# Two-operand sums made by accumulating DMA transfers from GpSimd instead of a tensor-tensor add

## The chip, the cores and the metric

The kernel runs on one core of a Trainium2 chip. Times are device microseconds (us) of that core, from the first to the last thing that the program does there. The engines are TensorE (PE in the profile; its weight loads are PEld), VectorE (DVE), ScalarE (ACT), GpSimd (POOL) and SyncE (SP), which issues the DMA transfers. Each engine works through its own list of instructions in order, and waits on semaphores that the others, or a landed transfer, raise.

## What is computed

Two independent layers of 2048 rows and width 1024, put side by side in the output. A is attention with 32 heads of 32 columns and a projection; B is a Fourier mixing by dense matrices, with the real part kept. All data is float32.

```python
def _A_ref(x, wqkv, wo):
    qkv = ((x @ wqkv).reshape(B, S, 3, H, Dh)).transpose(2, 0, 3, 1, 4)
    q, k, v = qkv[0], qkv[1], qkv[2]
    p = softmax(einsum("bhqd,bhkd->bhqk", q, k) * Dh ** -0.5)
    o = einsum("bhqk,bhkd->bhqd", p, v)
    return o.transpose(0, 2, 1, 3).reshape(B, S, D) @ wo

def _B_ref(x, dft_seq_re, dft_seq_im, dft_hid_re, dft_hid_im):
    a = einsum("bsd,ed->bse", x, dft_hid_re)
    b = einsum("bsd,ed->bse", x, dft_hid_im)
    return einsum("ts,bse->bte", dft_seq_re, a) - einsum("ts,bse->bte", dft_seq_im, b)

out = concatenate([_A_ref(...), _B_ref(...)], axis=-1)
```

## The kernel before

**The dense products.** Every dense product (QKV, the two Fourier products `dense1` and `dense2`, the projection) is done by a seven-product scheme on quarters of its operands, in the manner of Strassen and Winograd. The products are numbered 1 to 7, and each takes as operands a quarter or a signed sum of quarters. In QKV they run as products 1, 2, 5, 6, 3, then 7 and 4; in the others as `ORDER`, 1, 2, 6, 7, 5, 3, 4. Lists such as `w_terms`, `x_terms`, `a_terms` and `b_terms` give for each product the terms of an operand: a sign, a source in DRAM, and what has to have been written before. Product 5's stationary operand is `(+q10, +q11)`, product 6's is `(+q10, +q11, -q00)`. Of the moving operands, product 6's in `dense1` and `dense2` has a third term with a plus sign.

An operand is split into two float32r parts, high and low (`halves`: a cast at L527 on ACT or L528 on DVE, and a subtraction at L531 on POOL or DVE), and a product is three matmuls for each pair of tiles (L421, or L443 where three groups are interleaved).

**How an operand is fetched.** `fetch` (L465 and after) loads the first term into a tile `raw` (in the first stage `er`) of 128 x 512 float32, 256 KB, by a DMA on SP (L491). For every further term that lies in DRAM it loads a second tile `g` (in the first stage `raw`) by another DMA on SP (L500), and combines the two by one elementwise instruction, L507, which may go to POOL or to DVE. Then come the cast and the subtraction. Rings of buffers limit how far ahead the loads run: six `raw`, four `g`, four pairs of high and low for stationary operands.

**Attention.** For each head, scores are made twice: with queries on the partitions (`psS`, L1322) for the row maxima (DVE, L1328) and row sums (ACT, L1331), and transposed (`psT`, L1447), with an exponential on ACT (L1456), as the operand of the product with V (L1479). This goes on from about 240 us to about 2750 us, and the matmuls of the dense products are set between.

**The order.** The order of all engines is written out when the program is built, by a list scheduler, `Plan`. It plays the kernel through with assumed durations: it starts an operation when its operands are ready, charges a transfer 256 KB at 360 KB per us (`KB_US`) and 1.6 us more until it lands (`LANDING`), and lets POOL and DVE read a landed tile no sooner than 2 us after that (`MARGIN`). It also keeps POOL's elementwise instructions and those of DVE marked `two` from overlapping (`port`, `choose`), and where they come near each other adds a dependency (`behind`). PE takes dense matmuls where the attention has nothing ready, and in proportion to what is done of it. The plan fixes only the order; on the chip every instruction waits for what it needs.

Of the kernel before, what the change touches and what calls it, by code (L numbers as in the profile page):

```python
# [11 lines left out]
ALU = mybir.AluOpType  # L12
# [11 lines left out]
NB = 512  # L24
NPT, NPT2 = 23, 8
H2 = 8
NRAW, NHL, NG = 6, 4, 4
WARM = 10
NE, NCR = 4, 4
PEND = 1  # L30
# [36 lines left out]
class Plan:  # L67
# [26 lines left out]
    def op(self, engine, cost, emit, after=(), uses=(), rank=0.0, kb=0, order=None, other=None, lanes=1, two=False):  # L94

        o = Op(engine, cost, emit, rank, kb, other, two)
        o.lanes = lanes
        seen = set()  # L100
        for d in after:
            if d is not None and id(d) not in seen:
                seen.add(id(d))
                self._wait(o, d)
        for u in uses:
            u.append(o)
        if order is not None:
            p, order.first = order.first, o
            if p is not None and not p.begun:
                p.soon.append(o)  # L110
                o.left += 1
        if o.left == 0:
            self._release(o)
        return o

    def _wait(self, o, d):
        if d.end is None:
            d.then.append(o)
            o.left += 1
        else:  # L120
            o.ready = max(o.ready, self.after(d, d.engine, o))
            if d.engine == "SP":
                o.landed = max(o.landed, d.end)

    def after(self, d, e, o):
# [8 lines left out]
    def start(self, o, e=None):  # L134
        e = e or o.engine
        made = o.emit(e) if o.other else o.emit()
        o.begun = True
        self.free[e] = self.now + (o.cost if e == o.engine else o.other[1])
        if e == "POOL" or e == "DVE" and o.two:
            self.port = self.free[e]  # L140
        if e == "DVE" and o.two:
            self.held = made, self.free[e]
        elif e == "POOL" and self.held is not None and self.held[1] > self.now - self.NEAR:
            self.behind(made, self.held[0])
        if o.kb:
            for _ in range(o.lanes):
                t = max(self.free[e], self.lane[0])
                self.dma = max(self.dma, t) + o.kb / o.lanes / self.KB_US
                o.end = self.dma + self.LANDING
                self.lane = self.lane[1:] + [o.end]  # L150
                if o.lanes > 1:
                    self.free[e] = t + o.cost
        else:
            o.end = self.free[e]
            self.free[e] -= self.OVERLAP.get(e, 0.0)
        for t in o.then:
            t.ready = max(t.ready, self.after(o, e, t))
            if e == "SP":
                t.landed = max(t.landed, o.end)
            t.left -= 1  # L160
            if t.left == 0:
                self._release(t)
        for t in o.soon:
            t.ready = max(t.ready, self.now)
            t.left -= 1
            if t.left == 0:
                self._release(t)
        o.then = o.soon = ()
        o.emit = None
# [56 lines left out]
def kernel(  # L226
# [11 lines left out]
    nc = tc.nc  # L238
# [143 lines left out]
    NEAR = 0.2  # L382
    SFIRST = 0.3
    ADD = 0.68
    FILL = 3 * (7 * 24 * 4 + 7 * 16 * 4 + 7 * 8 * 16 + 2 * 8 * 4)
    ATT = H * (128 * MM + 16 * PV) + (3 * H2 + 2 * (H - H2)) * SWITCH

# [2 lines left out]
    op = pl.op  # L390
# [66 lines left out]
    def seq():  # L457
        return float(len(frees))
# [10 lines left out]
    def fetch(shape, terms, store=None, keep=None):  # L469

        box = {}
        raws, seconds, tile_of, gate = where[0]
        rank = seq()
        sign, *first = terms[0]
        loaded = len(first) == 2
        if len(terms) == 1 and not loaded:
            return first[0].get, first[0].made, first[0].users
        if keep is None:
            old, users = raws.take()
        else:  # L480

            old, users = gate + keep.users, keep.users

        def dest():
            if "r" not in box:
                box["r"] = tile_of(shape, "raw", len(raws.users)) if keep is None else keep.get()
            return box["r"]

        last = None
        if loaded:  # L490
            last = op("SP", ISSUE, lambda: nc.sync.dma_start(dest(), first[0]), old + first[1] + gate, [users], rank, 256, raws if keep is None else None)  # L491
            old = []
        for sign, *term in terms[1:]:
            other = {}
            if len(term) == 2:
                gold, gusers = seconds.take()

                def load(src=term[0], other=other):
                    other["q"] = tile_of(shape, "g", len(seconds.users))
                    nc.sync.dma_start(other["q"], src)  # L500

                q = op("SP", ISSUE, load, gold + term[1] + gate, [gusers], rank, 256, seconds)
            else:
                other["k"], q, gusers = term[0], term[0].made, term[0].users

            def add(e, sign=sign, other=other, a=None if last is not None else first[0]):
                return (nc.gpsimd if e == "POOL" else nc.vector).tensor_tensor(  # L507
                    out=dest(), in0=dest() if a is None else a.get(), in1=other["q"] if "q" in other else other["k"].get(), op=ALU.add if sign > 0 else ALU.subtract)

            last = op("POOL", SUB, add, old + [first[0].made if last is None else last, q], [users, gusers] + ([first[0].users] if last is None else []),  # L510
                      rank, 0, raws if keep is None and last is None else None, other=("DVE", ADD, 20 + rank), two=True)
            old = []
        if keep is not None:
            keep.made = last
        if store is not None:
            store[1].append(op("SP", ISSUE, lambda: nc.sync.dma_start(store[0], dest()), [last], [users], rank, 256))
        return dest, last, users
# [3 lines left out]
    def halves(raw, made, users, hi, lo, old, mine, order=(None, None)):  # L521
# [11 lines left out]
        a = op("DVE", CAST, high, [made] + old[0], [users, mine[0]], 10 + rank, 0, order[0], ("ACT", ACAST, 25 + rank) if spare[0] else None, two=True)  # L533
        b = op("POOL", SUB, low, [a] + old[1], [users, mine[0], mine[1]], rank, 0, order[1], other=("DVE", ADD, 25 + rank), two=True)
        return a, b

    def piece(terms, store=None):

        box = {}
        raw, made, users = fetch([P, 4, P], terms, store)  # L540
        (o0, u0), (o1, u1) = HR.take(), LR.take()

        def tile_of(key):
            def get():
                if key not in box:
                    box[key] = parts.tile([P, 4, P], F32R, name=key, tag=key, bufs=NHL)
                return box[key]
            return get

        h, l = tile_of("h"), tile_of("l")  # L550
        made = halves(raw, made, users, h, l, (o0, o1), (u0, u1), (HR, LR))
        both = Both(u0, u1)
        return Piece(h, l, made, both)
# [67 lines left out]
    def qkv():  # L621
# [128 lines left out]
        def gather(p, g, result, early, scale=None):  # L750
# [21 lines left out]
            def finish(ps, last):  # L772
# [43 lines left out]
                def put_u3(o):  # L816
                    if whole_u3:
                        u3[g] = (U2[0], U2[1], o)
                    else:
                        u_st[g][1].append(op("SP", ISSUE, lambda: nc.sync.dma_start(u_d[g][1], U2[0]()), [o], U2[1], rank, 256))  # L820

                if g < 2 * PAIRS or g >= 16:
                    def third(r, made, users):

                        o = op("POOL", SUB, lambda e: (nc.gpsimd if e == "POOL" else nc.vector).tensor_tensor(out=U2[0](), in0=r(), in1=U2[0](), op=ALU.subtract),
                               [made, U2[2]], [users, *U2[1]], rank, other=("DVE", ADD, 20 + rank), two=True)
                        put_u3(o)
# [130 lines left out]
    def add_op(emit, after, users, rank):  # L958
        return op("POOL", SUB, emit, after, users, rank, other=("DVE", ADD, 20 + rank), two=True)

# [595 lines left out]
    while nf < len(fills) or any(place[n] < len(s) for n, s in streams.items()):  # L1556
# [4 lines left out]
        if visit:  # L1561
            o = visit[0]
# [25 lines left out]
        for n, (o, h, k, *_) in heads.items():  # L1588
# [14 lines left out]
            rank = {"V": 0, "T": 1, "S": 0.5 if stock > SFIRST else 1.5}[n]  # L1603
            if n == "S" and "T" in heads and heads["T"][0].left == 0:
# [4 lines left out]
                if lead > 0:  # L1609
                    rank = 2  # L1610
            ok.append((rank, n))
        fill = None
        if nf < len(fills):
            o, first, left = fills[nf]
# [5 lines left out]
            elif ready < 1e17:  # L1620
                times.append(ready + LATE)
        if fill is not None and (not ok or (not first and left <= HB) or nf / (FILL - RES) <= done / ATT):
            pl.start(fill)
# [5 lines left out]
        if ok:  # L1629
            n = min(ok)[1]  # L1630
            o = heads[n][0]
# [48 lines left out]
```

## Time and profile before

| | us |
|---|---|
| three runs, median | 2942.45 |
| three runs, lowest to highest | 2941.8 to 2943.91 |
| profiled execution, span from first to last instruction | 2940.6 |
| PE busy in it | 2931.5 |
| DVE, ACT, POOL busy | 2275.1, 2271.7, 956.6 |

The page of the profile gives the profiled execution by its span alone; the runs' median lies 1.85 us above that span and the fastest run 1.2 us. The granted clock of TensorE is 1.000 throughout. The page's parts are read in this order: busy time by engine, the span in 40 slices, the DMA queues, the chain of work that ended last, then the groups of instructions by line.

### The profile page before, as it was taken

How to read it: one execution, taken by the hardware profiler on the slowest of the kernel's cores; microseconds unless marked ns; L12 is line 12 of the kernel's file. 1: busy time of each engine (PE TensorE's matmuls, PEld its weight loads, DVE VectorE, ACT ScalarE, POOL GpSimd, SP SyncE). 2: the span in 40 equal slices, each digit the busy share in tenths (PEclk: the TensorE clock that was granted, in tenths of full speed). 3: DMA queues.
4: the chain of work that ended last, by engine and by line, in shares of the span. 5: the costliest groups of instructions: out<-in, count | busy, mean ns of one | idle time of the engine just before them, and what ended most of it. 6: DMA issues, size and time to landing. Idle time of an engine off the chain costs nothing.

```text
span 2940.6 us, 45778 instructions
## 1 busy us (share of the span) xinstructions
PE 2931.5 (100%) x14922; PEld 2151.9 (73%) x14922; DVE 2275.1 (77%) x3103; ACT 2271.7 (77%) x4322; POOL 956.6 (33%) x746
## 2 busy tenths in 40 slices
PE   9999999999999999999999999999999999999999
PEld 7887777677777777777777777777777777677787
DVE  6778888788877877877677888787787788886685
ACT  5348888888888888888888888888888888886331
POOL 2323435222204432231112454433112454454142
PEclk9999999999999999999999999999999999999999
DMA  9975658666637655675434776655434786665753
GB/s 348 356 249 183 200 183 276 227 213 225 218 103 229 217 176 164 212 226 166 158 101 147 239 231 205 189 180 169 129 113 132 216 270 200 194 182 191 264 194 126
DMA packets 393880, 587.96 MB, mean 200 GB/s; under 512 B 112782, under 2 KB 114574, under 8 KB 393518
## 3 DMA queue, kind: packets, MB, share of 16 engines
q1 hardware_dynamic: 393644, 585.05, 61.8%
q8 instruction: 120, 1.97, 0.3%
q14 instruction: 116, 0.95, 0.1%
HBM read 421.30 MB, written 163.59 MB: 199 GB/s over the span
## 4 chain that ended last, share of the span: by engine, by line
PE 98%; DVE 1%; DMA 1%; ACT 0%; SPq 0%; issue 0%; DVEq 0%; ACTq 0%
PE pd L421 44%; PE psT L1447 16%; PE psS L1322 16%; PE pd L1479 15%; PE psT L421 6%; DVE negm L1328 0%; DMA er<-in_xa 0%; DVE l L531 0%; DMA qs<-qk_d 0%; PE psT L443 0%; ACT psS L1331 0%; DVE h L528 0%; PE pd L443 0%; ACT slot L527 0%; DVE slot L531 0%
## 5 line engine op out<-in xcount | busy, mean ns | idle before, releaser
L1328 DVE TENSOR_REDUCE negm<-psS 128x1 f32<-128x1024 f32 x1024 | 1242.8, 1221 | 226.4 <-PE psS L1322 215.2
L1331 ACT ACTIVATE psS<-psS,negm 128x1024 f32<-128x1024 f32 x1024 | 1223.9, 1195 | 71.8 <-DVE negm L1328 70.0
L421 PE MATMUL pd<-slot,h 128*128 128x512 f32 x3360 | 1144.0, 390 | 0.0
L1456 ACT ACTIVATE pt<-psT 128x512 f32<-128x512 f32 x1296 | 782.6, 697 | 260.1 <-PE psT L1447 237.2
L1447 PE MATMUL psT<-qs,ks 128*128 128x512 f32 x2048 | 794.3, 394 | 1.3 <-DMA qs<-qk_d 1.3
L421 PEld LDWEIGHTS pd<-slot,h 128*128 128x128 f32 x3360 | 630.7, 188 | 132.0
L421 PE MATMUL pd<-slot,l 128*128 128x512 f32 x1680 | 654.6, 390 | 0.0
L507 POOL TENSOR_TENSOR raw<-raw,g 128x512 f32<-128x512 f32 x295 | 382.6, 1304 | 483.8 <-DVE l L531 63.8
L1447 PEld LDWEIGHTS psT<-qs,ks 128*128 128x128 f32 x2048 | 381.8, 188 | 137.3 <-issue 45.3
L1322 PE MATMUL psS<-ks,qs 128*128 128x512 f32 x1552 | 473.4, 390 | 1.2 <-ACT psS L1331 1.2
L531 POOL TENSOR_TENSOR l<-raw,h 128x512 fp32r<-128x512 f32 x157 | 202.5, 1290 | 554.6 <-PE psT L1447 236.6
L531 POOL TENSOR_TENSOR slot<-raw,slot 128x512 fp32r<-128x512 f32 x156 | 201.0, 1293 | 518.0 <-DVE slot L528 146.3
L421 PEld LDWEIGHTS pd<-slot,l 128*128 128x128 f32 x1680 | 315.3, 188 | 67.0 <-issue 0.8
L1479 PE MATMUL pd<-pt,vt 128*32 128x512 f32 x2592 | 345.8, 594 | 0.0
L1322 PEld LDWEIGHTS psS<-ks,qs 128*128 128x128 f32 x1552 | 290.8, 188 | 64.0 <-ACT psS L1331 3.8
L1331 ACT ACTIVATION_READ_ACCUMULATOR psS<-psS,negm 128x1 f32 x1024 | 321.6, 314 | 0.0
L1456 ACT ACTIVATE ptm<-psT 128x512 f32<-128x512 f32 x392 | 242.6, 715 | 49.7 <-PE psT L1447 46.7
L1456 ACT ACTIVATE ptl<-psT 128x512 f32<-128x512 f32 x360 | 223.5, 708 | 31.0 <-PE psT L1447 30.2
L1479 PEld LDWEIGHTS pd<-pt,vt 128*32 128x32 f32 x2592 | 89.4, 110 | 180.3 <-issue 168.2
L421 PE MATMUL pd<-slot,slot 128*128 128x512 f32 x768 | 193.0, 391 | 0.0
L421 PEld LDWEIGHTS pd<-slot,slot 128*128 128x128 f32 x768 | 144.1, 188 | 31.2
L528 DVE CAST h<-raw 128x512 fp32r<-128x512 f32 x321 | 149.1, 467 | 14.5 <-PE pd L421 12.3
(139 smaller groups left out, 2323.8 us busy)
## 6 DMA issues: line engine op xcount, KB each, us to landing
raw<-in_ct SPq DMA_DIRECT2D x224, 256.0 KB
g<-in_ct SPq DMA_DIRECT2D x128, 256.0 KB
c<-u_d SPq DMA_DIRECT2D x120, 256.0 KB
qk_d<-e SPq DMA_DIRECT2D x52, 512.0 KB
qs<-qk_d SPq DMA_DIRECT2D x128, 192.0 KB
ks<-qk_d SPq DMA_DIRECT2D x128, 192.0 KB
raw<-ab_d SPq DMA_DIRECT2D x96, 256.0 KB
g<-ab_d SPq DMA_DIRECT2D x80, 256.0 KB
```

What stands on the lines that cost most here:

```text
L421: nc.tensor.matmul(box["ps"], a[1]((a[0].hi, a[0].lo)[u]()), b[1]((b[0].hi, b[0].lo)[v]()), start=k == 0, stop=k == n - 1)
L507: return (nc.gpsimd if e == "POOL" else nc.vector).tensor_tensor(out=dest(), in0=dest() if a is None else a.get(), in1=other["q"] if "q" i ...
L528: return nc.vector.tensor_copy(hi(), raw())
L531: return (nc.gpsimd if e == "POOL" else nc.vector).tensor_tensor(out=lo(), in0=raw(), in1=f(hi()), op=ALU.subtract)
L1322: nc.tensor.matmul(p[:, i * NB : i * NB + NB], (QX[0] if own else QS[h % 2])[:, qt * P : qt * P + P], KS[h % 2][:, c * 1024 + i * NB : c * ...
L1328: nc.vector.tensor_reduce(out=ST["negm"][:, c, qt : qt + 1], in_=box["p"], axis=AX.X, op=ALU.max, negate=True)
L1331: nc.scalar.activation(box["p"], box["p"], AF.Exp, bias=ST["negm"][:, c, qt : qt + 1], accum_out=ST["sums"][:, c, qt : qt + 1])
L1447: nc.tensor.matmul(box["p"], KS[h % 2][:, t * P : t * P + P], QS[h % 2][:, j * NB : j * NB + NB], start=True, stop=True)
L1456: nc.scalar.activation(box["t"], box["p"], AF.Exp)
L1479: nc.tensor.matmul(po["p"][j * DH : j * DH + DH, :], VT[h][:, k, :], box["t"], start=(k == t0), stop=(k == t), tile_position=(0, j * DH),)
```

## The change

In `fetch`, a further term that has a plus sign, lies in DRAM, and is added to a first term that was loaded too, no longer takes a tile of its own and an elementwise addition. GpSimd issues a DMA with `accum_op=add` from DRAM onto the first tile. The operation waits for the first tile's load (and for what wrote the term), and the later steps wait for its landing. Terms with a minus sign, and sums with a tile that is kept on the chip, stay as they were.

The scheduler learns the new kind of operation: it costs POOL 1.0 us (`DGE`), then counts as a transfer of 256 KB on the same DMA budget as SP's, without one of SP's eight lanes; it doesn't hold the port that POOL and DVE share, and no dependency of the `behind` kind is added for it. What follows it is treated as following a landed transfer.

Room: the ring of `g` tiles goes from four to three, and the space for descriptors of GpSimd's transfers from 256 to 1024 bytes of each partition.

```diff
-NRAW, NHL, NG = 6, 4, 4
+NRAW, NHL, NG = 6, 4, 3
@@ Plan._wait
-            if d.engine == "SP":
+            if d.kb:
                 o.landed = max(o.landed, d.end)
@@ Plan.start
-        if e == "POOL" or e == "DVE" and o.two:
+        if e == "POOL" and not o.kb or e == "DVE" and o.two:
             self.port = self.free[e]
...
-        elif e == "POOL" and self.held is not None and self.held[1] > self.now - self.NEAR:
+        elif e == "POOL" and not o.kb and self.held is not None and self.held[1] > self.now - self.NEAR:
             self.behind(made, self.held[0])
-        if o.kb:
+        if o.kb and e == "POOL":
+            self.dma = max(self.dma, self.free[e]) + o.kb / self.KB_US
+            o.end = self.dma + self.LANDING
+        elif o.kb:
...
-            if e == "SP":
+            if o.kb:
                 t.landed = max(t.landed, o.end)
@@ constants
+    DGE = 1.0
+    ACC = [True]
@@ fetch
             other = {}
+            if len(term) == 2 and sign > 0 and loaded and ACC[0]:
+                last = op("POOL", DGE, lambda src=term[0]: nc.gpsimd.dma_start(dest(), src, accum_op=ALU.add), [last] + term[1], [users], rank, 256)
+                continue
             if len(term) == 2:
                 gold, gusers = seconds.take()
@@ kernel
-    nc = bacc.Bacc("TRN2", target_bir_lowering=False, num_devices=1, dynamic_dma_scratch_size=256)
+    nc = bacc.Bacc("TRN2", target_bir_lowering=False, num_devices=1, dynamic_dma_scratch_size=1024)
```

## The prediction

> **What bounds the kernel now.** I read the page first (busy time, chain, DMA), then PE's own waits, then the table of stretches of 100 us and of 10 us, then the chain in order of time.
>
> ```profile
> span 2940.6 us, 45778 instructions
> PE 2931.5 (100%) x14922; PEld 2151.9 (73%) x14922; DVE 2275.1 (77%) x3103; ACT 2271.7 (77%) x4322; POOL 956.6 (33%) x746
> PE 98%; DVE 1%; DMA 1%; ACT 0%; SPq 0%; issue 0%; DVEq 0%; ACTq 0%
> ```
>
> PE is busy for 2931.5 of 2940.6 us and makes 98% of the chain. A busy PE need not be a PE at its pace, so I check that busy time hides no waiting:
>
> ```profile
> 2852.52 5.44 PE pd L421 x24
> 1970.98 7.00 PE pd L1479 x64
> L1479 PE MATMUL pd<-pt,vt 128*32 128x512 f32 x2592 | 345.8, 594 | 0.0
> L1479 PE MATMUL pd<-ptl,vt 128*32 128x512 f32 x720 | 136.8, 593 | 0.0
> L1479 PE MATMUL pd<-ptm,vt 128*32 128x512 f32 x784 | 125.5, 593 | 0.0
> L1555 PE MATMUL pd<-qs 96*128 96x512 f32 x10 | 4.6, 644 | 1.5 <-DVE qs L303 1.5
> ```
>
> In the last stage, where nothing but dense products is left, a matmul starts every 5.44 / 24 = 0.2267 us; a matmul with V starts every 7.00 / 64 = 0.1094 us. Of the 14922 matmuls, 2592 + 720 + 784 = 4096 are with V, 10 are a warm-up, and 10816 are of the first kind: 10816 x 0.2267 + 4096 x 0.1094 = 2452.0 + 448.1 = 2900.1 us. The warm-up is 4.6 us, and the plan's own price of changing to the products with V, 0.363 us for each of 8 x 3 + 24 x 2 = 72 visits, makes 26.1 us. Together 2930.8 of the 2931.5 us busy. PE runs at its pace, and the change takes no matmul away.
>
> So only PE's idle time, 2940.6 - 2931.5 = 9.1 us, can be won. Where does it lie?
>
> ```profile
> 0.00:10.00 10.00, 8.54 (x27) 6.61 (x28) 4.02 (x7) 5.27 (x8) 5.68 (x8) 1.00 0.75 241
> 10.00:20.00 10.00, 8.67 (x37) 6.58 (x37) 9.10 (x16) 8.94 (x15) 1.28 (x1) 1.00 0.96 341
> 2900.00:2940.00 40.00, 36.84 (x163) 30.18 (x161) 13.47 (x20) 2.51 (x4) 2.62 (x3) 1.00 0.26 99
> PE psT L443 <- DVE acc L799: 1.3, 1, 1.3
> PE psT L1447 <- DMA qs<-qk_d: 1.3, 1, 1.3
> PE psS L1322 <- ACT psS L1331: 1.2, 3, 0.5
> ```
>
> The columns of a stretch are its length, then busy us (and count) of PE, PEld, DVE, ACT, POOL, then granted clock, DMA share and GB/s. The first 20 us lose 1.46 + 1.33 = 2.8 us, before any sum that the change touches is wanted (they belong to products 5 and 6; the first products are 1 and 2). The end loses 3.2 us, the last result's way out, and 0.6 us past 2940. That leaves 9.1 - 2.8 - 3.2 - 0.6 = 2.5 us in between: the second and third of these waits, 1.3 + 1.2. The change can gain at most these 2.5 us, less than a tenth of a per cent. What it can lose isn't bounded so.
>
> **The change, part by part.** A difference of 0.2%, 5.9 us, is about what a measurement of this kernel can tell from none.
>
> How many sums: the rule takes terms with a plus sign behind a loaded first term. Products 5 and 6 have one each in a stationary operand: QKV 8 weight blocks x 2 and 4 value blocks x 2 = 24; `dense1` 8 x 2 = 16; `dense2` 2 halves x 16 tiles x 2 = 64. The moving operand of product 6 has one: 8 in `dense1`, 16 in `dense2`. The projection has none (its plus terms go with tiles kept on chip). Sum 24 + 16 + 64 + 24 = 128. Of them 7 + 7 = 14 fall in QKV's first stage (3 weight blocks and 4 value blocks for each product), 114 beside the attention.
>
> *Removed: 128 additions at L507.*
>
> ```profile
> 0.00:2940.00 2940.00, 110.01 (x146) 407.35 (x314) 1.00 0.62 200
> L507 POOL TENSOR_TENSOR raw<-raw,g 128x512 f32<-128x512 f32 x295 | 382.6, 1304 | 483.8 <-DVE l L531 63.8 <-issue 48.2 <-DMA raw<-in_xb 44.9
> L500 SPq DMA_DIRECT2D g<-in_ct x128: 327/376/1986, 1600.7 to 2580.3; - x128
> ```
>
> In the first row stand busy us (and count) of DVE and of POOL at L507. There are 146 + 314 = 460; at the same shares, 128 are about 87 on POOL (87 x 1.297 = 113 us) and 41 on DVE (41 x 0.753 = 31 us). On engines busy 33% and 77% of the span, beside a PE that doesn't wait for them, that is worth nothing. SP issues 128 loads fewer, at 0.376 us median 48 us of its time; also off the path.
>
> *Added: 128 issues on POOL.* GpSimd issues no transfer in this trace, so the price is bounded: from below by an issue on SP, 0.33 us, from above by POOL's own pass over such a tile, 1.30 us. I take 1.0, the plan's price, which lies by the upper row. That is 128 us, against 113 removed; nothing on the path.
>
> *Added: one more read on the DMA engines.* A sum reads the tile it writes: 128 x 256 KB = 33.6 MB.
>
> ```profile
> q1 hardware_dynamic: 393644, 585.05, 61.8%
> 1700.00:1800.00 100.00, 100.00 (x521) 72.96 (x513) 81.46 (x108) 85.04 (x165) 50.68 (x39) 1.00 0.70 219
> 2300.00:2400.00 100.00, 100.00 (x505) 73.86 (x504) 84.46 (x111) 89.05 (x171) 55.74 (x44) 1.00 0.78 246
> 110.00:120.00 10.00, 10.00 (x46) 8.29 (x45) 5.31 (x10) 4.11 (x7) 2.05 (x2) 1.00 0.99 337
> 150.00:160.00 10.00, 10.00 (x45) 8.26 (x45) 5.99 (x9) 2.72 (x5) 3.81 (x3) 1.00 0.74 246
> ```
>
> Beside 585 MB it is 6% (nothing, if the read costs no time of its own; 61.8% to 65.4%, if it costs as a write does). In the attention's heaviest stretches, products 5 and 6 of `dense2`, the engines stand at 0.70 and 0.78, and it is hidden. In the first 150 us they stand at about 1.0: a rival, below.
>
> *Moved: the sum from "two loads side by side, then an add" to "a load, then a transfer".* In the plan the cast may start, after the first load has landed and 2 us passed, 1.0 + 256/360 + 1.6 + 2.0 = 5.3 us later, against 1.3 us or 0.7 us for an addition. POOL waits for the first load at the head of its queue, and behind it stand the low halves (L531) and the subtractions; it waits so now as well (44.9 us before L507 for `in_xb` alone). The tile is held about 4 us longer in a ring of six; at 24 operands in about 100 us of a product each of the six may be held 25 us. `g` going from four to three costs nothing where half of the stationary operand's seconds no longer use it.
>
> *The wait that counts* is that of the cast on DVE, because behind it stand the row maxima, for which ACT waits, which frees `psS`, for which PE waits. Now:
>
> ```profile
> L528 DVE CAST slot<-raw 128x512 fp32r<-128x512 f32 x228 | 103.1, 466 | 8.7 <-DMA raw<-ab_d 4.4 <-POOL raw L507 3.8
> L507 DVE TENSOR_TENSOR raw<-raw,g 128x512 f32<-128x512 f32 x77 | 55.5, 728 | 3.3 <-POOL raw L507 1.8 <-DMA g<-in_ct 1.3 <-issue 0.2
> ```
>
> DVE waits 4.4 + 3.8 + 1.8 + 1.3 = 11.3 us for loads and sums, and PE waits 1.2 us on ACT's `psS`: about 0.11 us of PE for each us of DVE. That is an estimate from few cases, but the only one here. I take it that one in eight of the 114 transfers comes 1 us too late for its cast: 14 us of DVE, 14 x 0.11 = 1.5 us of PE.
>
> Sum: 2940.6 (span) + 1.85 (what the median of the runs stands above it) + 1.5 = 2944.0 us. Ends: -2.5 (all waits go) to what the first rival costs.
>
> **The rivals.**
>
> *Sums land late* (slower). Place: products 5 and 6 of `dense1` and `dense2`. If a transfer takes on average more than the plan's 5.3 us, the cast stalls DVE each time. The nearest rows to a transfer's length, and to DVE and POOL getting into each other's way:
>
> ```profile
> 8.77 4.66 DMA er<-in_xa
> 119.25 1.30 POOL L531 TENSOR_TENSOR slot<-er,slot 128x512 fp32r<-128x512 f32 x1 [5.76 <-ACT slot L527]
> 119.73 1.37 DVE L531 TENSOR_TENSOR l<-er,h 128x512 fp32r<-128x512 f32 x1 [1.75 <-ACT h L527]
> ```
>
> A wait for a load of 4.66 us, on nearly full DMA engines, with an issue of 1.30 is 6.0 us, 0.7 late. Where POOL and DVE meet, the DVE subtraction took 1.37 instead of the 0.69 us of the next row quoted; the plan no longer keeps the new issues and DVE's `two` instructions apart, and a stretch of 0.68 us may fall on either. Twice the load (9.3), with issue and stretch (2.0), is 11.3 us, 6.0 late. Price: 114 x lateness x 0.11. It passes 5.9 us from a mean lateness of 0.47 us; 1 us gives 12.5 us, 2955; 2 us gives 25 us, 2967. Against it: POOL is idle two thirds of the time and issues as soon as the load has landed, up to 2 us ahead of the plan, so the allowance is nearer 7 us than 5.3; and DMA engines at 0.6 to 0.78 are quicker than at 0.96.
>
> The Trainium skill ("SBUF — State Buffer", section "SBUF: two separate sides") speaks for this rival: it says that GpSimd can't write descriptors while DVE holds the shared port, and tells of a transfer of about 620 ns that took about 3100 ns. By an estimate from that page, 2.5 us on each transfer would give 114 x 2.5 x 0.11 = 31 us, 2974. This trace's meeting of POOL and DVE agrees in kind, with 0.68 us; DVE's holders last 0.47 to 0.75 us here, so I don't take the page's size.
>
> *The full DMA engines of the first stage.* Product 6's third weight block is ready late already:
>
> ```profile
> 129.62 0.69 DVE L531 TENSOR_TENSOR l<-er,h 128x512 fp32r<-128x512 f32 x1 [2.47 <-ACT h L527]
> 135.30 0.39 PE L421 MATMUL pd<-slot,l 128*128 128x512 f32 x1
> ```
>
> Its low half ends at 130.3 and is used at 135.3, 5.0 us later. If the extra read costs as much as a load, 14 x 262 kB at the 337 GB/s of 110 to 120 us, 0.78 us each, puts transfers back by 10.9 us, and PE stalls 5.9 us: 2948. Against it: the share falls to 0.74 by 150 us, and other operands are further ahead.
>
> The Trainium skill ("Collectives: The Full Stack", section "The bandwidth ceiling: the fold count and why AG ≠ RS ≠ AR") says that an addition in the DMA path needs two source reads and runs at half the rate of a copy. No transfer of this trace adds, so it can't be weighed here; by it the sum would be this rival's.
>
> *All waits go*: 2942.45 - 2.5 = 2940, within the bound. *Faster by more* needs time that the trace doesn't show as idle. *Nothing is replaced*: the rule matches the terms counted above, so no chance is given; it would give 2942.
>
> **How the numbers follow.** Fed as now, up to 5.9 us worse: 0.58, the forecast, 2944.0. All waits go: 0.10. Sums land late: 0.22. First stage: 0.07, of which 0.02 within the bound. Faster by over 5.9 us: 0.03. Same 0.58 + 0.10 + 0.02 = 0.70; slower 0.22 + 0.05 = 0.27; faster 0.03. The range goes from 2938.5, a little below "all waits go", to 2960, a mean lateness of about 1.4 us; about 0.1 lies above.
>
> **What would show it.** L507 falls by 128 to 332 and SP's loads of `g` and of the first stage's second tiles by 128; POOL has 128 issues. PE's busy time stays at 2931 to 2932. If I am right, PE's waits between 20 and 2900 us stay under 8 us, and DVE's waits on the summed tiles under 60 us in all. If sums land late, DVE's casts wait over 60 us for a transfer and PE's `psS` waits grow along; if it is the first stage, PE idles between 90 and 170 us. It would also be wrong if the list scheduler, given other costs, puts PE's work in an order in which it waits for something that this change doesn't touch.

## The result, and the profile after

| kernel | median us | lowest to highest | runs |
|---|---|---|---|
| before | 2942.66 | 2941.8 to 2943.91 | 4 |
| after | 2964.59 | 2960.21 to 2966.48 | 4 |

The ratio is 1.0073, with a 95% interval of 1.0059 to 1.0088. The change costs 22 us: less than one per cent, but clear of the noise, and above the range of the prediction. The profiled execution after has a span of 2963.7 us, 23.1 us above the 2940.6 of before.

The page after: span, busy time by engine, the two DMA queues (packets, MB, share of 16 engines) and the chain by engine.

```profile
span 2963.7 us, 45606 instructions
PE 2941.9 (99%) x14922; PEld 2148.7 (73%) x14922; DVE 2241.7 (76%) x3052; ACT 2277.0 (77%) x4320; POOL 973.1 (33%) x799
...
q1 hardware_dynamic: 375212, 551.49, 58.0%
q0 software_dynamic: 18432, 33.56, 6.9%
...
PE 90%; DMA 5%; DVE 2%; issue 1%; ACT 1%; POOL 1%; SPq 0%; DVEq 0%; POOLq 0%; ACTq 0%
```

PE still makes most of the chain, but 5% of it is now DMA. PE's idle time went from 9.1 to 2963.7 - 2941.9 = 21.8 us, and its busy time grew by 10.4 us with the same 14922 matmuls.

GpSimd's transfers after, by source (duration of the issue in ns, lowest, median, highest; first and last start; the first and the last of seven groups, 128 issues in all), and the time from issue to landing of all of them:

```profile
L501 POOL DMA_DIRECT2D raw<-in_ct x64: 849/882/1509, 1631.7 to 2618.1; - x64
...
L501 POOL DMA_DIRECT2D er<-in_wqk x6: 867/884/1234, 54.8 to 131.8; - x6
...
DMA to landing us min/median/max: 3.6/6.5/9.9
```

The additions that are left after (the same view as the first row for L507 of before, now L515; DVE, then POOL):

```profile
0.00:2963.00 2963.00, 69.35 (x90) 318.22 (x242) 1.00 0.65 198
```

90 + 242 = 332: 128 additions are gone and 128 transfers are there, as counted. Issuing one takes 0.88 us. But a transfer that adds takes the DMA engines 6.9% of the span for 33.56 MB, 0.206% for each MB, where SP's transfers take 58.0 / 551.49 = 0.105%. An added byte costs 1.96 times one that SP's transfers move.

**Where PE loses the time.** PE's waits after (us in total, times, longest us):

```profile
PE psS L1330 <- ACT psS L1339: 8.2, 13, 1.4
PE psS L1330 <- DMA ks<-qk_d: 4.3, 2, 3.2
PE psT L1455 <- DMA qs<-m_d: 1.7, 2, 0.9
...
```

There are two places. The second row belongs to one stall, in the first stage, with a single matmul between its two waits. Here are the stretches of 10 us there (columns as in the prediction), before:

```profile
60.00:70.00 10.00, 10.00 (x45) 8.27 (x45) 5.93 (x9) 1.87 (x3) 0.76 (x1) 1.00 1.04 384
70.00:80.00 10.00, 10.00 (x46) 8.26 (x44) 7.75 (x10) 6.24 (x12) 5.14 (x4) 1.00 1.00 350
80.00:90.00 10.00, 10.00 (x46) 8.28 (x45) 6.07 (x10) 3.08 (x6) 5.17 (x4) 1.00 1.03 383
```

and after:

```profile
60.00:70.00 10.00, 10.00 (x46) 8.28 (x45) 5.56 (x10) 3.68 (x6) 2.17 (x3) 1.00 1.07 352
70.00:80.00 10.00, 5.70 (x18) 4.05 (x17) 4.50 (x6) 2.42 (x5) 2.49 (x2) 0.76 1.04 382
80.00:90.00 10.00, 10.00 (x42) 8.14 (x40) 6.74 (x9) 4.52 (x9) 3.41 (x3) 0.90 1.01 339
```

The DMA share (last column but one) is 1.0 and more in both: there is no room for a second read. From 60 to 90 us PE starts 106 matmuls instead of 137; 31 x 0.2267 = 7.0 us. The other way to count: PE waits 4.3 us, and the granted clock of 0.76 and 0.90 takes 2.4 + 1.0 = 3.4 us. In stretches of 1 us the clock is 0.61 from 75 to 76 us and 0.50 from 76 to 82; PE was still waiting up to 76.75, so about 0.8 of the 3.4 us fall into the wait and must not be counted twice. That gives 4.3 + 2.6 = 6.9 us, the same. What PE waited for is in the chain up to 80 us after (start, length, what):

```profile
54.82 8.77 DMA er<-in_wqk
...
63.62 0.64 ACT h L535
...
66.26 0.64 ACT vh L535
...
67.07 5.49 DMA qk_d<-e
...
72.62 4.09 DMA ks<-qk_d
...
76.75 1.65 PE psS L1330 x3
```

An accumulating transfer of product 5's weights takes 8.77 us to land. ACT, which works in order, waits for it with the cast at 63.62, and the cast at 66.26 that belongs to the store of queries and keys comes behind. The store and the load of the keys themselves take 5.49 and 4.09 us more. So the first head's keys come back at 76.7, and PE has meanwhile run out of dense matmuls. In the prediction this rival stood at another operand, at 130 us.

The rest, 23.1 - 7.0 = 16 us, is lost beside the attention. The waits view shows 8.2 - 1.2 = 7.0 us of it as waits for `psS`; the remainder is in short waits and in busy time that stretched. Part of the stretch shows at the weight loads (PEld), whose waiting PE's busy time covers: they waited 3.9 us for `psS` before and 17.2 us after. How much of these 13.3 us PE lost isn't shown. The stretches that the prediction called the heaviest, after:

```profile
1700.00:1800.00 100.00, 96.94 (x507) 66.00 (x509) 76.22 (x97) 80.44 (x154) 59.18 (x49) 1.00 0.78 229
2300.00:2400.00 100.00, 98.39 (x526) 67.44 (x525) 76.58 (x110) 82.28 (x159) 51.24 (x46) 1.00 0.83 224
```

The share rose from 0.70 and 0.78 to 0.78 and 0.83, still well under 1, and PE, which was busy for all of both before, idles 3.1 and 1.6 us. A mean over 100 us hides what a transfer meets. The last 30 us of the second stretch before, in stretches of 10 us:

```profile
2370.00:2380.00 10.00, 10.00 (x52) 7.54 (x45) 6.94 (x8) 8.18 (x16) 6.54 (x5) 1.00 0.97 316
2380.00:2390.00 10.00, 10.00 (x46) 8.25 (x45) 8.37 (x10) 10.00 (x21) 7.25 (x6) 1.00 0.99 310
2390.00:2400.00 10.00, 10.00 (x44) 7.76 (x43) 9.81 (x13) 9.85 (x19) 6.16 (x6) 1.00 0.93 313
```

and the first 30 us of the first one after:

```profile
1700.00:1710.00 10.00, 9.24 (x40) 6.69 (x39) 9.31 (x10) 9.02 (x19) 6.55 (x6) 1.00 1.02 294
1710.00:1720.00 10.00, 10.00 (x80) 4.45 (x78) 4.46 (x7) 6.11 (x13) 6.44 (x6) 1.00 0.90 243
1720.00:1730.00 10.00, 9.13 (x41) 6.49 (x37) 8.27 (x9) 7.29 (x14) 6.46 (x7) 1.00 0.91 233
```

Before, 1700 to 1730 us stands at 0.93, 0.73 and 0.90. Where the engines have most to do they were nearly full already before, and full or nearly so after. A full stretch alone doesn't make PE idle, though: before, PE is busy through those at 0.93 to 0.99. How a full stretch becomes idle time is seen in one case after, in the timelines of SP, POOL, DVE, ACT and PE (start, length, engine, line, operation; in brackets the idle time before it and what ended it):

```profile
1713.31 0.43 SPq L508 DMA_DIRECT2D g<-ab_d  x1
...
1712.86 2.67 POOL L501 DMA_DIRECT2D raw<-in_ct  x3
1714.58 2.26 POOL L539 TENSOR_TENSOR l<-raw,h 128x512 fp32r<-128x512 f32 x1
1718.78 2.53 POOL L515 TENSOR_TENSOR raw<-raw,g 128x512 f32<-128x512 f32 x2 [1.93 <-DMA g<-ab_d]
...
1721.34 0.43 DVE L536 CAST slot<-raw 128x512 fp32r<-128x512 f32 x1 [6.84 <-POOL raw L515]
...
1723.01 2.35 DVE L1336 TENSOR_REDUCE negm<-psS 128x1 f32<-128x1024 f32 x2
...
1724.32 1.09 ACT L1339 ACTIVATE psS<-psS,negm 128x1024 f32<-128x1024 f32 x1 [1.20 <-DVE negm L1336]
...
1725.58 0.73 PE L1330 MATMUL psS<-ks,qs 128*128 128x512 f32 x2 [0.87 <-ACT psS L1339]
```

Read from the end: PE waits for ACT to free `psS`, ACT for a row maximum, the row maximum stands on DVE behind a cast, the cast waits 6.84 us for a sum that POOL makes. It isn't one of the 128: POOL adds a `g` that is an ordinary load by SP, issued at 1713.31 and not in before 1718.78, amid three accumulating transfers that POOL issues from 1712.86 on. But only 1.93 of the 6.84 us are POOL's wait for this load. Ahead of it POOL issues the three transfers and makes a low half in 2.26 us (1.28 us for the one at 1705 us), and behind it come two additions, 2.53 us, after which the cast starts. So late loads and POOL's own queue both show in this case, and it can't say which is the cause.

### The profile page after: what moved, and what is told of

It is laid out like the page before. It is cut to its first block, busy times and chain, and to the rows that moved or that the text cites. A ratio compares the mean times of both kernels' runs of the same rounds, so it can differ in the third digit from the quotient of the medians.

```text
span 2963.7 us, 45606 instructions
## 1 busy us (share of the span) xinstructions
PE 2941.9 (99%) x14922; PEld 2148.7 (73%) x14922; DVE 2241.7 (76%) x3052; ACT 2277.0 (77%) x4320; POOL 973.1 (33%) x799
## 3 DMA queue, kind: packets, MB, share of 16 engines
q1 hardware_dynamic: 375212, 551.49, 58.0%
q0 software_dynamic: 18432, 33.56, 6.9%
## 4 chain that ended last, share of the span: by engine, by line
PE 90%; DMA 5%; DVE 2%; issue 1%; ACT 1%; POOL 1%; SPq 0%; DVEq 0%; POOLq 0%; ACTq 0%
PE pd L426 40%; PE psT L1455 15%; PE psS L1330 15%; PE pd L1487 14%; PE psT L426 6%; DVE negm L1336 1%; DMA raw<-in_ct 1%; DMA g<-in_ct 1%; DMA raw<-in_xb 0%; ACT psS L1339 0%; DMA g<-ab_d 0%; DMA er<-in_wv 0%; DMA qs<-qk_d 0%; POOL raw L515 0%; DMA er<-in_wqk 0%
## 5 line engine op out<-in xcount | busy, mean ns | idle before, releaser
L515 POOL TENSOR_TENSOR raw<-raw,g 128x512 f32<-128x512 f32 x222 | 292.4, 1326 | 398.1 <-DMA raw<-in_wd 53.5
L426 PEld LDWEIGHTS pd<-slot,l 128*128 128x128 f32 x1680 | 315.4, 188 | 65.4
L1339 ACT ACTIVATION_READ_ACCUMULATOR psS<-psS,negm 128x1 f32 x1024 | 311.9, 305 | 0.0
```

The lines of the kernel that those rows point to most:

```text
L426: nc.tensor.matmul(box["ps"], a[1]((a[0].hi, a[0].lo)[u]()), b[1]((b[0].hi, b[0].lo)[v]()), start=k == 0, stop=k == n - 1)
L1339: nc.scalar.activation(box["p"], box["p"], AF.Exp, bias=ST["negm"][:, c, qt : qt + 1], accum_out=ST["sums"][:, c, qt : qt + 1])
```

## The experiments

**The theory:** the second read takes the DMA engines' time, and that delays the transfers near it, SP's plain loads too. **The rivals:** each sum itself comes late for its cast (the plan allows too little); issuing on POOL costs; or another order and one `g` less cost. The first of these rivals was the theory at the start: "theory" in the expectations of e_later, e_first, e_copy and e_long means it, and the result of e_long, below, spoke against it. Each kernel is the changed one with the edit shown (e_tiny's is shown against e_traffic); where operands have two shapes, the diff shows one. Before's median and the ratio are of the same chip.

| run | median us | lowest to highest (runs) | before, us | ratio, interval |
|---|---|---|---|---|
| e_later | 2959.46 | 2952.73 to 2967.14 (4) | 2941.54 | 1.0063, 1.0044 to 1.0082 |
| e_first | 2951.00 | 2949.72 to 2952.84 (5) | 2941.54 | 1.0034, 1.0021 to 1.0047 |
| e_copy | 2946.48 | 2944.09 to 2949.86 (10) | 2941.54 | 1.0018, 1.0008 to 1.0027 |
| e_long | 2968.69 | 2966.45 to 2970.46 (4) | 2941.54 | 1.0093, 1.0078 to 1.0108 |
| e_none | 2944.12 | 2942.31 to 2945.62 (10) | 2941.99 | 1.0007, 0.9997 to 1.0016 |
| e_traffic | 2962.57 | 2960.26 to 2963.36 (5) | 2941.99 | 1.0069, 1.0056 to 1.0082 |
| e_plan2 | 2954.91 | 2952.57 to 2955.95 (5) | 2941.99 | 1.0043, 1.0029 to 1.0057 |
| e_long_later | 2958.18 | 2954.81 to 2960.17 (5) | 2941.99 | 1.0053, 1.0040 to 1.0066 |
| e_light | 2953.22 | 2950.53 to 2959.66 (5) | 2942.79 | 1.0039, 1.0026 to 1.0051 |
| e_slow | 3021.57 | 3018.42 to 3024.65 (5) | 2942.79 | 1.0267, 1.0253 to 1.0281 |
| e_tiny | 2946.88 | 2943.34 to 2949.98 (11) | 2941.80 | 1.0015, 1.0006 to 1.0024 |

**Which sums cost: e_later (the 114 beside the attention) and e_first (the 14 of the first stage).**

```diff
-            if len(term) == 2 and sign > 0 and loaded and ACC[0]:
+            if len(term) == 2 and sign > 0 and loaded and raws is RAW:      # e_later
+            if len(term) == 2 and sign > 0 and loaded and raws is not RAW:  # e_first
```

> Accumulating transfers only from the second half of QKV on (114 of 128); the first stage adds as before. Theory (sums land later than the plan allows, 6.5 us against 5.3, and hold up what stands behind their casts, in the first stage and beside the attention): the first stage's 8 us go, the attention's 15 us stay, 2942.7 + 15 = 2956 to 2959, and PE doesn't idle between 60 and 100 us. Rival 1 (it is the full DMA engines of the first stage alone): 2943 to 2945. Rival 2 (the smaller ring of g and the order that the list scheduler then makes, not the transfers): near the changed kernel, 2962 to 2966.

> Accumulating transfers only in the first stage (14 of 128). Theory: the first stage's idle time and slowed clock stay, 2942.7 + 8 = 2949 to 2952; from 250 us on PE waits as in the kernel before (under 4 us). Rival 1 (first stage alone): 2960 to 2966. Rival 2 (ring and order): anything from 2950 to 2966, with waits beside the attention although nothing is accumulated there.

With the 114 alone the time is 17.9 us above before, with the 14 alone 9.5 us. Two rows, first e_later's stretch from 70 to 80 us:

```profile
70.00:80.00 10.00, 10.00 (x46) 8.29 (x45) 7.79 (x10) 6.28 (x12) 5.14 (x4) 1.00 1.02 359
```

and then PE's longest wait in e_first:

```profile
PE psS L1330 <- DMA ks<-qk_d: 4.3, 2, 3.3
```

The stall on the first head's keys comes with the 14 and goes without them. Both halves cost; 14 early sums cost half as much as 114 later ones, and e_later came out just above what was expected. The two don't add up exactly to 22 (each has an order of its own), and e_later spreads over 14 us, so its part is known only roughly.

**Is it the order and the rooms? e_none.** No sum is made by a transfer; three `g` and the larger space for descriptors stay.

```diff
-    ACC = [True]
+    ACC = [False]
```

> The changed kernel without accumulating transfers: three g tiles and 1024 bytes for descriptors stay, the sums are added as before. Theory (the transfers are the cost): as the kernel before, 2940 to 2946. Rival (room and order are the cost): 2950 or more.

2.1 us above before, a tenth of the loss, with an interval that contains no change and reaches to 1.0016, 4.7 us. The order here isn't the changed kernel's own, since the plan orders additions and no transfers; that order is kept in the next run.

**Is it the addition in the transfer? e_copy.** The same transfer from the same place in the same order, without the addition, so the sums are not formed.

```diff
-nc.gpsimd.dma_start(dest(), src, accum_op=ALU.add)
+nc.gpsimd.dma_start(dest(), src)
```

> The changed kernel with the same order of every engine, but GpSimd's 128 transfers copy instead of adding (the additions are left out, so the sums hold only their last loaded term). Theory A (it is the time from issue to landing): the packets take about half (85 instead of 178 ns), landing comes 1 to 1.5 us sooner, 5 to 5.5 us, which is about what the plan allows, so most of the loss goes: 2944 to 2952. Rival (it is GpSimd's issue, its descriptors and its place in POOL's queue, not the addition): landing and time stay, 2960 to 2966.

17 of the 22 us are gone: 4.9 us above before remain. The queues on e_copy's page:

```profile
q1 hardware_dynamic: 375212, 551.49, 58.8%
q0 software_dynamic: 10240, 33.56, 3.6%
```

and GpSimd's transfers in it, the largest group and the landing:

```profile
L501 POOL DMA_DIRECT2D raw<-in_ct x64: 536/553/608, 1621.9 to 2596.0; - x64
...
DMA to landing us min/median/max: 2.9/4.7/7.3
```

The same bytes take 3.6% instead of 6.9% of the engines. But three things changed at once: engine time, the sum's own landing (6.5 to 4.7 us) and the issue (0.88 to 0.55 us). The next runs part them.

**Engine time put back without the addition: e_traffic.** e_copy, and beside each copy SP issues a plain transfer of the same 256 KB from DRAM to a spare place in DRAM, which nothing reads. The sums are not formed here either.

```diff
+dump = [dram.tile([P, NB], F32, name=f"dump{i}") for i in range(16)]
...
-nc.gpsimd.dma_start(dest(), src, accum_op=ALU.add)
+(dump.append(dump.pop(0)), nc.sync.dma_start(dump[0], src), nc.gpsimd.dma_start(dest(), src))[2]
```

> e_copy (GpSimd's transfers copy, the additions are left out) with 128 more transfers of 256 KB from DRAM to DRAM issued on SP beside them, for which nobody waits: about the DMA engines' time that accumulating takes in addition, but not on the sums' own path. The order of the other instructions stays. If the loss comes from the sums' own way from issue to landing: 2946 to 2950, near e_copy, as long as GpSimd's transfers still land within about 5.3 us. If it comes from the time taken from the other transfers on the DMA engines: 2955 to 2964, with DVE and POOL waiting longer for SP's loads.

2962.57 is 20.6 us above before: 16 of the 17 us are back. The queues on its page:

```profile
q1 hardware_dynamic: 390956, 585.05, 62.0%
q0 software_dynamic: 10240, 33.56, 3.5%
```

and PE's two longest waits in it:

```profile
PE psS L1330 <- ACT psS L1339: 6.4, 9, 2.0
PE psS L1330 <- DMA ks<-qk_d: 3.2, 1, 3.2
```

The engines are taken for 62.0 + 3.5 = 65.5% of the span, after for 64.9%. Both of PE's stalls return in the same two places, though the copies land after 5.5 us in the median, nearer to e_copy's 4.7 than to 6.5, and POOL issues as in e_copy. The stall on the keys comes here by way of plain transfers: in the chain up to 80 us stand two stores to `qk_d`, 6.47 and 5.06 us, and the load of `ks`, 4.18 us.

Who waits longer can be summed from the waits views of the runs that share one order. POOL waited for landed transfers 381 us in e_copy, 449 in after and 459 in e_traffic; without those for GpSimd's own transfers it is 361, 423 and 410, so SP's plain transfers do hold POOL up longer. DVE waited for GpSimd's transfers 9.0 us in e_copy, 25.7 in after and 16.6 in e_traffic, so these come later too when the engines are taken.

**Is it SP's extra issues? e_tiny.** e_traffic with the side transfer cut to 16 x 128, 8 KB; SP issues as many. The sums are not formed.

```diff
-nc.sync.dma_start(dump[0], src)
+nc.sync.dma_start(dump[0][0:16, 0:P], src[0:16, 0:P])
```

> e_traffic with the 128 transfers beside cut from 256 KB to 8 KB each (the additions are still left out): SP issues as many instructions in the same order, the DMA engines have almost none of the extra work. If e_traffic lost by the DMA engines' time: near e_copy, 2945 to 2949, and PE doesn't idle between 60 and 100 us. If it lost by 128 more issues in SP's queue: near e_traffic, 2958 to 2963.

```profile
q1 hardware_dynamic: 379308, 552.54, 58.6%
...
```

This is SP's queue on e_tiny's page: against e_copy, 128 issues more and hardly a byte more. The ratio is 1.0015, as e_copy's 1.0018. So it was the engine time of e_traffic, not its issues. One part of the expectation was missed: between 60 and 100 us PE idled 1.1 us.

**The other way: keep the additions, take other traffic away. e_light.** The changed kernel, whose loads of `g` fetch only a quarter of their columns; the remaining additions use that quarter four times, so those sums have other values.

```diff
-                    nc.sync.dma_start(other["q"], src)
+                    nc.sync.dma_start(other["q"][:, 0:P], src[:, 0:P])
```

> The changed kernel with its accumulating transfers, in the same order, but the loads of g that are left on SP from the second half of QKV on fetch a quarter of their columns (192 of 256 KB less each, some 300 of them), and the additions repeat that quarter: the sums are left wrong by that. It takes about as much time from the DMA engines beside the attention as the additions in flight put there; the first stage is untouched. If the loss beside the attention is DMA engine time: its 15 us go, the first stage's 8 us stay, 2949 to 2954, though accumulating stays the slow way from issue to landing. If it is the sums' own way: 2958 to 2965.

It stands 10.4 us above before, half of what after does. SP's queue on its page:

```profile
q1 hardware_dynamic: 375212, 501.55, 52.6%
```

and PE's waits in it:

```profile
PE psS L1330 <- ACT psS L1339: 3.9, 6, 0.8
PE psS L1330 <- DMA ks<-qk_d: 3.3, 1, 3.3
```

With 5.4 points of engine time freed, more than the 3.3 that the second reads take, the waits for `psS` fall from 8.2 to 3.9 us, although GpSimd's transfers still add, still take 6.9% and still hold POOL 0.88 us each. The first stage, whose second tiles are not of that ring, keeps its stall. The reading has a limit: the lighter loads also bring the ordinary additions forward, so this run alone would not part "late loads" from "late sums".

**Would a better informed plan help? e_long, e_plan2, e_long_later.** The plan is told that such a transfer lands later, or takes twice the engines' time as well, for all sums or for the 114 alone.

```diff
-            o.end = self.dma + self.LANDING
+            o.end = self.dma + self.LANDING + 3.2                             # e_long, e_long_later
...
-            self.dma = max(self.dma, self.free[e]) + o.kb / self.KB_US
+            self.dma = max(self.dma, self.free[e]) + 2 * o.kb / self.KB_US    # e_plan2, with LANDING + 2.5
...
-            if len(term) == 2 and sign > 0 and loaded and ACC[0]:
+            if len(term) == 2 and sign > 0 and loaded and raws is RAW:        # e_plan2, e_long_later
```

> The changed kernel with one number of the plan changed: a transfer of GpSimd's counts as landing 3.2 us later (6.5 us after its issue instead of 3.3, the median measured). Theory: the casts then stand in the order where their data is there, DVE and ACT don't stall on them, 2943 to 2949. Rival (the transfers themselves are the cost, by DMA engines or by POOL): no better than 2958.

> Accumulating from the second half of QKV on, as in e_later, and the plan charges such a transfer twice the DMA time and lets it land 6.5 us after its issue. If the loss is that the plan knows neither the landing nor the engines' time: 2943 to 2949. If the additions in flight cost PE whatever the plan says (e_long speaks for it): 2953 to 2962, as e_later.

> Accumulating from the second half of QKV on, with only the landing 3.2 us later in the plan. If e_long lost in the first stage alone what it won beside the attention: 2943 to 2949. If a right landing time doesn't help beside the attention, because there it is the other loads that come late: 2953 to 2962.

If the sums only came later than planned, this should cure most of it. e_long is slower than after, against what was expected:

```profile
PE psS L1330 <- ACT psS L1339: 8.9, 13, 2.6
PE pd L426 <- ACT h L535: 4.0, 2, 3.4
```

In these rows of PE's waits in e_long the attention's stalls are as they were, and the first stage waits for weights as well. For the 114 sums the two forms give 2954.91 and 2958.18 against 2959.46 without; e_later's own spread covers both, so at most a few us come from it.

**A late sum without engine time: e_slow, which doesn't tell.** e_copy with GpSimd held for a while ahead of each transfer, by a small copy and eight memsets. The sums are not formed.

```diff
-nc.gpsimd.dma_start(dest(), src, accum_op=ALU.add)
+(nc.gpsimd.tensor_copy(junk[:, 0:8], dest()[:, 0:8]), [nc.gpsimd.memset(junk, 0.0) for _ in range(8)], nc.gpsimd.dma_start(dest(), src))[2]
```

> e_copy (GpSimd's transfers copy, the additions are left out) with a copy of eight columns and eight memsets of 128 columns on POOL ahead of each, after the first load has landed: about 1.7 us more from the load's landing to the sum's, as accumulating had it, and no more DMA traffic. If the loss is the sums' own lateness: 2956 to 2964. If it is the DMA engines' time: 2946 to 2951.

3021.57: far more than either theory gave. The memsets' group in it:

```profile
L501 POOL MEMSET junk<- 128x128 f32 x1024 | 221.4, 216 | 59.1
```

They take 221.4 + 59.1 us of POOL, and the small copies 28.7 us more: 309 us, 2.4 us for each of 128 transfers. Everything behind them in POOL's queue is late as well, the low halves and the other additions, and that costs 78.8 us over before, 74 us more than e_copy. So it delays far more than the sum and doesn't part the two theories; a late sum without engine time stays untested. It does show that POOL, busy a third of the time, has no slack in the right places.

**What follows.** With everything else in the same order, the loss follows the engines' time: 3.6% of the span for these transfers gives 4.9 us, 6.9% gives 22, and 3.5% with as much again put beside it gives 20.6. So as much engine time, put back by plain transfers, is enough for some 16 of the 22 us, and taking engine time away from other traffic takes much of the loss away. The sum's later landing by itself and the longer issue aren't needed for it: e_traffic lands 1.0 us earlier in the median and issues in 0.55 us. Two things stay open. Engine time reaches PE through late plain loads and through late sums, and the runs don't part these two ways. And the longer issue of the adding transfer, 0.33 us for each of 128, may carry a part of its own: an estimate at e_slow's rate (74 us for 309) is 10 us, which e_light, with the same issue and little loss beside the attention, speaks against. The 4.9 us of e_copy hold its order, its issues and its landings together. No version here was faster than before.

## Why the prediction was wrong

- **What bounds the kernel: right.** PE was the bound and at most 2.5 us were to be had. That left only a loss, which the forecast put at 1.5 us.
- **The count: right.** 128 sums, 14 of them in the first stage, 332 additions left. Taken off POOL and DVE they were worth nothing, as said.
- **The issue on POOL: right in size.** 0.88 us in the median against 1.0. The rule of the Trainium skill ("SBUF — State Buffer", section "SBUF: two separate sides") was weighed against it: a transfer of 3100 ns. None of the 128 issues is over 1.7 us, so no such stretch shows on POOL. Whether a part of the 6.5 us to the landing is of that kind, no run here shows.
- **One more read on the DMA engines: the step that failed.** The prediction put the engines' share in the heaviest stretches at 0.70 and 0.78 "and it is hidden", and set it to nothing. Its size was bounded well (61.8 to 65.4% for the engines' share; it came to 64.9%), and the rule on two source reads that stood beside it ("Collectives: The Full Stack" of the Trainium skill, section "The bandwidth ceiling: the fold count and why AG ≠ RS ≠ AR") agrees with the 1.96 times measured. What was wrong is that a share below 1 hides it. The 0.78 is a mean over 100 us, with 0.93 to 0.99 in the last 30 of them, before the change already; and a transfer that is late there holds up POOL, DVE, ACT and PE, which work their lists in order. The step was set to nothing; e_traffic puts its price at some 16 us over the whole kernel, the stall in the first stage with it.
- **The landing: too short.** The cast's allowance was 5.3 us from the issue, or nearer 7 by the prediction's argument that POOL issues early; the median is 6.5. The prediction took one in eight as 1 us late. Against 5.3 the median is 1.2 us late, and the rival "sums land late" would price that at 114 x 1.2 x 0.11 = 15 us, close to the 16 us lost beside the attention. That agreement is luck: e_traffic's copies are 0.2 us late by the same count, 2.5 us, and it lost nearly as much.
- **The price of a wait on DVE: too low.** It was 0.11 us of PE for each us, from 1.2 / 11.3. The 11.3 us are those of two rows; all of DVE's waits for transfers and for POOL's results came to 23.6 us in 19 cases before and 58.0 us in 37 after. 7.0 us more of PE's waits for `psS` over these 34.4 is 0.20, and the 16 us lost beside the attention over them is 0.47. So DVE's waits stayed under the 60 us that were to show the forecast right (DVE's casts waited 18.6 us for transfers), and the time was lost all the same.
- **The rival of the first stage: right in kind, wrong in place.** The full engines there did make PE stall, but at 72 us on the first head's keys, by way of ACT's queue, and not at 130 us on product 6's weights. The stall of 5.9 us in its price stands against some 7 us lost by 90 us, 4.3 of waiting and 2.6 of a lower clock, which was not in it.
- **Two signs showed it wrong:** PE's busy time left 2931 to 2932, and its waits between 20 and 2900 us passed 8 us (15.2).

## What to carry to other kernels

An addition in the DMA path took the DMA engines about twice as long as a load here, and the transfers near it came later. Before calling such time hidden, don't go by a mean share over 100 us: look at stretches as short as a few transfers (10 us here), and at what waits in order for the tiles that land there. Neither share decides it alone: a mean of 0.7 to 0.8 was not free here, while PE stayed busy through 10 us at 0.99 before. To test such a suspicion, take the addition away and put the same traffic back by other means, in the same order.

## What was unexpected of the hardware

- With a short stall the granted clock falls. At the stall of 72 to 77 us (waits of 1.1 and 3.2 us, one matmul between them) the rows for 70 to 90 us lose 3.4 us of clock, that is 6.8 us at half; it fell before the second wait was over and was back at 82 us. In e_long a stall of 2.6 us was enough; this is its stretch there:

```profile
2415.00:2430.00 15.00, 12.38 (x48) 9.72 (x47) 12.77 (x12) 11.47 (x24) 7.82 (x7) 0.89 0.91 251
```

  15 x 0.11 = 1.65 us of clock, 3.3 us at half, all of it after the wait. The Trainium skill ("TensorE: Matmul & The Clock Gate", section "HAM oscillation — how this bites in real kernels") warns of idle gaps over about 3.4 us. It agrees in kind; the single waits shown here are a little shorter.
- Issuing a transfer that adds takes POOL 0.88 us, one that copies 0.55 us, for the same tile.
- POOL is idle for two thirds of the span, and yet 309 us more in its queue cost 74 us.
